# A fused linear-attention and highway kernel: two tiles per GpSimd instruction, casting value loads, sigmoid for the last nine tiles, and a new order of steps

## The chip, the cores and the metric

The kernel runs on one NeuronCore of one Trainium2 chip. The metric is device time in microseconds of one execution. Inside the profile the span is counted from the first to the last instruction or transfer of the program; the execution's own time is a little longer than its span.

The engines are named as the profile names them: PE is TensorE (matmul), DVE is VectorE, ACT is ScalarE, POOL is GpSimd and SP is SyncE, which here does nothing but issue transfers.

## What is computed

```python
def _attn_ref(q, k, v):                    # each (8, 8, 576, 64), float32
    q_s = softmax of q over the last axis  # 64 channels
    k_s = softmax of k over axis 2         # 576 positions
    kv = einsum('bhsd,bhse->bhde', k_s, v)
    return einsum('bhsd,bhde->bhse', q_s, kv)

def _moe_ref(x, w_h, w_t, b_t):            # x (4608, 512), weights (512, 512)
    H = maximum(x @ w_h, 0)
    T = 1 / (1 + exp(-(x @ w_t + b_t)))
    return T * H + (1 - T) * x

x = attention output, (batch, position) by (head, channel)
```

Both softmaxes are written here in short. The output is float32, 4608 by 512.

## The kernel before

There are eight batches. Each has 576 rows, that is four and a half tiles of 128 rows. A pair of batches is cut into five groups: two groups of two tiles for each batch, and one group of a single tile that takes the last 64 rows of both. So there are 20 groups (u = 0 to 19) and 36 tiles (i = 0 to 35).

For a batch b the steps are: load q, k and v in float32 (`q`, `k`, `v`); exponentials of k and q on ACT to 16 bit (`ek`, `eq`); a cast of v to 16 bit on ACT, DVE or POOL (`vc`); the 72 small matmuls of k by v with a column of ones beside v that gives the sum (`kv`); reciprocal and scaling (`kr`, `kn`); a swap of row blocks on PE and its copy (`kp`, `kc`); and 32 by 32 transposes of the exponentials of q on DVE (`tr`).

For a group: the product with the query side on PE (`xu`), the reciprocals of its sums (`rs`) and the scaled rows x in 16 bit (`x`), both on DVE.

For a tile: four PE transposes (`xt`) and their copy out (`xe`); the bias put into a PSUM bank (`bw`, by a PE matmul, or by an ACT copy with `:A`); four matmuls with w_t on top of it (`mt`); four matmuls with w_h into another bank (`mh`); tanh of half the gate (`th`; with `:S` it stays in PSUM); then `dd` (L391), `gg` (L396), `uu` (L405 on POOL, L402 on DVE) and `oo` (L417) make the output row, and `st` or `st1` stores it. PSUM has three banks for gate and product (`ps_g`), four for `xu` and `kv`, and one for the transposes, of which half is used.

Before the change w_h has the identity taken off and is halved (`whd`, `whc`, L202 to L210), so that `dd` is max(half of H's product, minus half x) and the gate is tanh + 1.

What sets the order of all work is `ORDER`, one list of steps written out (L16 to L57). The program walks it once, and each step issues its instructions in that place on its engine's queue. Every engine runs its own queue in this order and waits only where data or a buffer is missing. All loads of q, k, v and the weights are issued by SP (L178, L184, L189), so they lie in one queue; the bias alone is loaded from ACT's queue (L192). The list begins:

```python
q_0_0_8 b_0 setupdve fill_10 b_32 v_0_1_1 bsplit bp fill_12 bc v_0_3_1 setuppool v_0_2_1 vc_0_2_1:A vc_0_1_1:D k_0_0_2
ek_0_0_2 perm bw_0_0 v_0_0_1 vc_0_0_1:P k_0_2_2 ek_0_2_2 w_t_2 wtc_2:P eq_0_0_8 vc_0_3_1:D kv_0 kr_0 kn_0 tr_0_0_8
fill_4 kp_0 kc_0:A q_0_8_10 bw_2_0 xu_0 rs_0 x_0 fill_5 xt_1 eq_0_8_10 tr_0_8_8 bw_1_0 w_t_0 wtc_0:P w_h_0 xe_1:A
whd_1:P xu_1 w_h_2 xt_0 rs_1 whd_2:P mt_1_0 th_1_0 xe_0:D mt_0_0 k_1_2_2 v_1_2_2 vc_1_2_2:P th_0_0 gg_0_0:P x_1 xt_2
xe_2:A mt_2_0 ek_1_2_2 th_2_0 whd_0:D k_1_0_2 ek_1_0_2 whd_3:D whc_2:D tr_0_16_2 whc_0:D mh_2 dd_2 mh_1 mh_0 bw_3_0
```

`fill_n` are n matmuls on zeros. The number after a load's batch is its first part and then how many parts: a whole k, v or q of one batch is 1,152 KB, a whole weight matrix 1,024 KB.

Of the kernel before, what the change touches and what calls it, by code (L numbers as in the profile page):

```python
# [8 lines left out]
FP32 = mybir.dt.float32  # L9
FP16 = mybir.dt.float16  # L10
# [11 lines left out]
gg_2_0:P uu_2_0:P oo_2_0:P xt_3 dd_1 v_1_0_2 vc_1_0_2:A kv_1 dd_0 gg_1_0:P q_1_0_8 eq_1_0_8 xe_3:D kr_1 mh_3 q_1_8_10
kn_1 kp_1 mt_3_0 kc_1:A v_3_0_4 tr_1_0_8 xu_2 dd_3 rs_2 x_2 xt_5 uu_0_0:P oo_0_0:P eq_1_8_10 bw_5_0 tr_1_8_8 xu_3
xe_5:D rs_3 th_3_0 xt_4 gg_3_0:P uu_1_0:P tr_1_16_2 uu_3_0:P oo_1_0:P vc_3_0_2:A mt_5_0 vc_3_2_2:P xe_4:A q_3_0_18 x_3
mh_5 k_3_0_4 dd_5 bw_4_0 xt_7 th_5_0 bw_7_0 eq_3_0_8 eq_3_8_10 mt_4_0 xe_7:D tr_3_0_8 th_4_0 xu_4 rs_4 xt_6 ek_3_0_4
gg_5_0:P mt_7_0 x_4 th_7_0 uu_5_0:P mh_4 mh_7 oo_3_0:P gg_4_0:P xe_6:D kv_3 gg_7_0:P oo_5_0:D mh_6 dd_4 k_2_0_4 dd_7
# [34 lines left out]
def kernel(  # L61
# [13 lines left out]
    P = 128  # L75
# [404 lines left out]
```

## Time and profile before

| what | us |
|---|---|
| runs, median (lowest to highest) | 122.46 (122.06 to 124.19) |
| the profiled execution's own time | 122.67 |
| its span | 120.9 |
| PE, DVE, POOL, ACT busy | 104.6, 95.1, 90.1, 88.5 |

The mean granted TensorE clock was 0.979 in the profiled execution. A row of the profile's groups names the line, engine and operation, what is written and read, the shape, and how often; then the busy time, the mean length of one in ns, and the idle time before it. The list of instructions in order of time has start and length in us. A row marked SPq is the time that SP took to issue a transfer, not the transfer.

### The profile page before, as it was taken

The numbers are of one execution on the slowest core, as the hardware profiler recorded it, in microseconds if no ns is written. First come the engines' busy times: TensorE is split into PE (matmuls) and PEld (weight loads), VectorE is DVE, ScalarE is ACT, GpSimd is POOL, SyncE is SP. The second block draws the span as 40 slices with busy tenths as digits, with TensorE's granted clock in tenths as the row PEclk, the third lists the DMA queues.
The fourth block names the chain that finished last, engine by engine and source line by source line (L and its number), as shares of the span: only waits on it lengthen the run. The fifth ranks groups of instructions, "written<-read, shape, count | busy, mean of one in ns | idle before, by whom it ended". The sixth has DMA issues, their size and how long they took to land.

```text
span 120.9 us, 4081 instructions
## 1 busy us (share of the span) xinstructions
PE 104.6 (87%) x1722; PEld 53.4 (44%) x1722; DVE 95.1 (79%) x171; ACT 88.5 (73%) x120; POOL 90.1 (75%) x102
## 2 busy tenths in 40 slices
PE   6993998886798999979999999999995999999900
PEld 2241543452453654345555454564552555444500
DVE  5430588569959899999988799999988699978860
ACT  4046644986599997889999999999977687767310
POOL 7002341798999899999649998969799999848930
PEclk9999779999999999999999999999999999999997
DMA  3999999999999999999999999999996442282442
GB/s 60 387 374 408 421 395 392 392 392 403 399 391 390 402 406 400 387 393 387 406 418 400 410 394 419 397 403 409 410 371 267 160 173 96 100 329 89 173 167 96
DMA packets 14886, 40.11 MB, mean 332 GB/s; under 512 B 914, under 2 KB 1170, under 8 KB 14868
## 3 DMA queue, kind: packets, MB, share of 16 engines
q1 hardware_dynamic: 14576, 39.59, 84.9%
q8 instruction: 13, 0.21, 0.7%
q10 hardware_dynamic: 292, 0.27, 0.7%
q14 instruction: 5, 0.04, 0.1%
HBM read 30.41 MB, written 9.44 MB: 330 GB/s over the span
## 4 chain that ended last, share of the span: by engine, by line
PE 49%; DMA 26%; ACT 10%; DVE 4%; SPq 3%; issue 2%; POOLq 1%; DVEq 0%
PE tps L371 19%; PE gps L377 17%; DMA k<-in_k_dram 13%; DMA w32h<-in_moe_w_h_dram 9%; PE turned L351 5%; DMA v<-in_v_dram 4%; ACT qe L285 4%; PE kv L254 3%; PE xu L316 3%; SPq L184 3%; ACT ek L235 2%; ACT v L240 2%; PE tps L366 1%; ACT tps L384 1%; ACT xT L357 1%
## 5 line engine op out<-in xcount | busy, mean ns | idle before, releaser
L377 PE MATMUL gps<-w16h,xT 128*128 128x512 f16 x144 | 36.2, 379 | 1.3 <-issue 1.3
L371 PE MATMUL tps<-w16t,xT 128*128 128x512 f16 (+1 forms) x148 | 36.4, 374 | 0.8 <-ACT xT L357 0.8
L417 POOL TENSOR_TENSOR o<-u,x 128x512 f32<-128x512 f16 x27 | 32.4, 1209 | 0.9
L405 POOL TENSOR_TENSOR u<-g,d 128x512 f16<-128x512 f16 (+1 forms) x25 | 28.7, 1150 | 3.7 <-DVE d L391 2.0
L391 DVE SCALAR_TENSOR_TENSOR d<-x,gps 128x512 f16<-128x512 f16 x36 | 24.2, 678 | 4.5 <-PE gps L377 3.6
L344 DVE TENSOR_TENSOR x<-xu,rs 128x1024 f16<-128x1024 f32 (+1 forms) x20 | 22.2, 1112 | 0.6
L303 DVE STREAM_TRANSPOSE et<-qe 128x512 f32<-128x512 f32 (+1 forms) x24 | 19.6, 835 | 2.4 <-ACT qe L285 2.2
L235 ACT ACTIVATE ek<-k 128x2304 f16<-128x2304 f32 (+1 forms) x10 | 18.9, 1893 | 2.4 <-DMA k<-in_k_dram 2.4
L396 POOL TENSOR_SCALAR g<-th 128x512 f16<-128x512 f16 (+1 forms) x25 | 16.0, 641 | 6.0 <-ACT th L387 3.3
L285 ACT ACTIVATE qe<-q 128x1024 f16<-128x1024 f32 (+1 forms) x16 | 18.4, 1160 | 2.4 <-DVE et L303 1.8
L377 PEld LDWEIGHTS <-xT 128*128 128x128 f16 x144 | 13.0, 98 | 14.0 <-issue 1.8
L371 PEld LDWEIGHTS <-xT 128*128 128x128 f16 x148 | 13.2, 98 | 12.7 <-ACT xT L357 0.9
L387 ACT ACTIVATE th<-tps 128x512 f16<-128x512 f32 (+1 forms) x25 | 14.5, 586 | 4.3 <-PE tps L371 4.2
L357 ACT COPY xT<-turned 128x512 f16<-128x512 f16 x23 | 13.4, 583 | 5.7 <-PE turned L351 5.7
L351 PE MATMUL turned<-idh,x 128*128 128x128 f16 x144 | 14.0, 220 | 2.6 <-DVE x L344 2.3
L240 POOL CAST v<-v 128x1152 f16<-128x1152 f32 (+1 forms) x8 | 9.0, 1131 | 8.9 <-DMA v<-in_v_dram 8.9
L351 PEld LDWEIGHTS <-x 128*128 128x128 f16 x144 | 10.0, 98 | 10.1 <-DVE x L344 3.9
L165 PE MATMUL turned<-blank 128*128 128x512 f16 x31 | 10.5, 500 | 1.2 <-DVE blank L153 1.2
L364 ACT COPY tps<-ball 128x512 f32<-128x512 f32 x17 | 10.0, 591 | 0.9 <-DVE d L391 0.8
L240 ACT CAST v<-v 128x1152 f16<-128x1152 f32 (+1 forms) x8 | 8.7, 1106 | 1.5 <-DMA v<-in_v_dram 1.5
L254 PE MATMUL kv<-v,ek 64*64 64x65 f16 x576 | 6.6, 193 | 3.2 <-ACT ek L235 1.9
L402 DVE SCALAR_TENSOR_TENSOR u<-tps,d 128x512 f16<-128x512 f32 (+1 forms) x12 | 7.9, 659 | 1.5 <-ACT tps L384 1.4
(50 smaller groups left out, 92.2 us busy)
## 6 DMA issues: line engine op xcount, KB each, us to landing
out_dram<-o SPq DMA_DIRECT2D x16, 512.0 KB, 9.8
v<-in_v_dram SPq DMA_DIRECT2D x6, 1152.0 KB, 15.2
q<-in_q_dram SPq DMA_DIRECT2D x6, 1152.0 KB, 15.2
k<-in_k_dram SPq DMA_DIRECT2D x6, 1152.0 KB, 17.8
k<-in_k_dram SPq DMA_DIRECT2D x4, 576.0 KB, 8.8
q<-in_q_dram SPq DMA_DIRECT2D x2, 640.0 KB, 12.4
v<-in_v_dram SPq DMA_DIRECT2D x4, 288.0 KB, 4.7
v<-in_v_dram SPq DMA_DIRECT2D x2, 576.0 KB, 12.3
```

The source lines that it names most:

```text
L235: nc.scalar.activation(dst[:, at], src[:, at], AF.Exp)
L240: copy(v16[b % NV][:, c:c + n, :, 0:D], src[:, c:c + n])
L285: nc.scalar.activation(t[:, :, j * D:(j + n) * D], src[:, :, j * D:(j + n) * D], AF.Exp)
L303: nc.vector.transpose(dst, src)
L344: nc.vector.tensor_mul(dst[:, :, 0:n], sums(u)[:, :, :, 0:64], T[f"rs{u}"][:, :, 0:n].unsqueeze(3).to_broadcast([P, 4, n, D]))
L351: nc.tensor.matmul(t[:, n], x_of(i)[:, n0 + n % 2:n0 + 2 * P:2], idh, is_transpose=True, start=True, stop=True, skip_group_check=True)
L371: nc.tensor.matmul(T[f"tps{i}_{h}"][:, cs], T[f"xT{i}"][:, n], w16["t"][:, n, cs], start=False, stop=(n == 3), skip_group_check=True)
L377: nc.tensor.matmul(t, T[f"xT{i}"][:, n], w16["h"][:, n], start=(n == 0), stop=(n == 3), skip_group_check=True)
L391: nc.vector.scalar_tensor_tensor(t, x_of(i), -0.5, T[f"gps{i}"], op0=ALU.mult, op1=ALU.max)
L396: nc.gpsimd.tensor_scalar(t[:, cs], T[f"th{i}_{h}"][:, cs], 1.0, 1.0, op0=ALU.add, op1=ALU.mult)
L405: nc.gpsimd.tensor_mul(t[:, cs], T[f"g{i}_{h}"][:, cs], T[f"d{i}"][:, cs])
L417: eng.tensor_add(t[:, cs], T[f"u{i}_{h}"][:, cs], x_of(i)[:, cs])
```

## The change

1. GpSimd's three steps can take both tiles of a group in one instruction (`gq`, `uq`, `oq`; 128 by 1024 in place of twice 128 by 512). To this end the intermediate tiles and the transposed x are allocated in pairs, two (or three) pairs deep, and the transposes of a group's two tiles go to the two halves of their PSUM bank. Seven of the gate steps go to ACT (`gg:A`, `gq:A`).
2. The weights are cast and nothing more. `dd` is now max(H, 0) minus x, the gate is half of tanh plus a half, and from tile 27 on ACT computes the sigmoid itself, so that these tiles have no gate step. A step `tab` runs one element column of sigmoid ahead of them.
3. The values of batches 2 to 7 are loaded by GpSimd's queue in float32 to 16 bit, the cast done by the transfer, into two buffers; a block of 64 ones behind the values takes the place of the column beside them, so the matmuls of k by v move 128 columns in place of 65 for these batches.
4. The query exponentials of batches 2 to 7 are one instruction of 2304 elements each. The x of four groups is made in two halves (`x:H`, `xb`).
5. The whole list of steps is a new one. The bias goes into PSUM by ACT in 29 cases (17 before) and by PE in 8 (20 before). Transposed tiles are copied out by DVE in 20 single steps and two double ones (13 before) and by ACT in 12 (23 before). On DVE lie 7 `uu` (12 before) and 9 `oo` (10 before).

```diff
 ORDER = """
...
+q_0_0_8 b_32 b_0 setupdve fill_10 v_0_1_1 v_0_3_1 v_0_0_1 bsplit v_0_2_1 k_0_2_2 vc_0_3_1:P k_0_0_2 w_t_2 q_0_8_10
+w_t_0 k_1_2_2 v_1_0_2 vc_0_2_1:A vc_0_0_1:D ek_0_2_2 v_1_2_2 bp fill_12 k_1_0_2 ek_0_0_2 q_1_0_8 w_h_2 setuppool w_h_0
+perm bc q_1_8_10 eq_0_0_8 k_2_0_4 wc_t_2:P vc_0_1_1:D kv_0 fill_3 kr_0 kn_0 kp_0 fill_2 q_2_0_18 v_2_0_4 tr_0_0_8
+kc_0:A xu_0 rs_0 bw_1_0:A x_0 eq_0_8_10 q_3_0_18 k_3_0_4 bw_0_0 fill_5 xt_0 xe_0:D wc_t_0:A mt_0_0 vc_1_2_2:P tr_0_8_8
+ek_1_2_2 v_3_0_4 xt_1 xe_1:D xu_1 rs_1 th_0_0 x_1 mt_1_0 th_1_0 ek_1_0_2 tr_0_16_2 k_4_0_4 xt_2 xe_2:D bw_3_0 wc_h_2:P
+bw_2_0 mt_2_0 xt_3 xe_3:A eq_1_0_8 vc_1_0_2:D kv_1 kr_1 kn_1 tr_1_0_8 kp_1 kc_1:A wc_h_0:D th_2_0 mt_3_0 th_3_0 xu_2
+rs_2 x_2 gg_2_0:P mh_1 dd_1 mh_0 gq_0:A dd_0 eq_1_8_10 tr_1_8_8 mh_2 xt_4 bw_5_0:A xe_4:D gg_3_0:P xt_5 xe_5:A uq_0:P
+mh_3 dd_2 xu_3 rs_3 mt_5_0 th_5_0 x_3:H uu_2_0:P tr_1_16_2 mh_5 xb_3:H xt_6 xu_4 bw_4_0 dd_3 mh_4 dd_5 rs_4 ek_2_0_4
+xt_7 xe_6:D x_4 eq_2_0_18 mh_6 uu_3_0:P mt_4_0 th_4_0 xe_7:D dd_6 oq_0:P bw_7_0:A kv_2 v_4_0_4 xt_8 xe_8:A dd_4 mt_7_0
+th_7_0 tr_2_0_8 kr_2 kn_2 gq_2:P uq_2:P tr_2_8_8 q_4_0_18 kp_2 kc_2:A tr_2_16_2 mh_7 dd_7 xu_5 mh_8 bw_8_0:A mt_8_0
...
+xe_34:A uu_32_0:P oo_32_0:D mt_33_0 st_12 xu_19 uu_31_0:P oo_26_0:P dd_28 mh_33 st_16 oo_31_0:D uu_28_0:D rs_19
+th_33_0 mh_34 bw_34_0:A mt_34_0 th_34_0:S oo_28_0:D x_19 dd_33 dd_34 xt_35 bw_35_1 uu_27_0:P xe_35:D st1_26_0
+uu_34_0:D oo_34_0:D mh_35 dd_35 oo_27_0:P uu_33_0:P st_17 st_15 bw_35_0 oo_33_0:P mt_35_1 th_35_1:S st_18 uu_35_1:D
+oo_35_1:P st1_35_1:A mt_35_0 th_35_0:S uu_35_0:D oo_35_0:D st1_35_0:A
 """
...
+    def load_v(e, b, c, n):
+        if b < CASTS:
...
+            nc.sync.dma_start(t[:, c:c + n], rows_of(v, b)[:, c:c + n])
+            return
+        w = NJ * D
+        t = v16s[b % NVS][:, c * w:(c + n) * w].rearrange("p (c f) -> p c f", c=n)
+        nc.gpsimd.dma_start(t, rows_of(v, b)[:, c:c + n])
...
+    def w_cast(e, w, c):
+        copy = dict(A=nc.scalar.copy, D=nc.vector.tensor_copy, P=nc.gpsimd.tensor_copy)[e]
+        copy(w16[w][:, c:c + 2], T[f"w{w}{c}"])
...
+                        at, vt = (NJ * i + j) * D, v16s[b % NVS]
+                        moving = bass.AP(vt.tensor, vt[rows, at:at + D].offset,
+                                         [list(vt[rows].ap[0]), [4 * NJ * D - at, 2], [1, D]])
...
-        t = T[f"xtps{i}"] = turned[:, 0]
+        t = turned[:, tiles[i][1]]
...
+        how = dict(func=AF.Sigmoid) if i >= SIGMOID else dict(func=AF.Tanh, scale=0.5)
...
-        nc.vector.scalar_tensor_tensor(t, x_of(i), -0.5, T[f"gps{i}"], op0=ALU.mult, op1=ALU.max)
+        nc.vector.scalar_tensor_tensor(pair("d", i), T[f"gps{i}"], 0.0, x_of(i), op0=ALU.max, op1=ALU.subtract)
...
+    def halved(e, g, th):
+        if e == "A":
+            nc.scalar.activation(g, th, AF.Identity, scale=0.5, bias=half)
+        else:
+            nc.gpsimd.tensor_scalar(g, th, 0.5, 0.5, op0=ALU.mult, op1=ALU.add)
...
+    def gq(e, g):
+        halved(e, both("g", g), both("th", g))
+
+    def uq(e, g):
+        nc.gpsimd.tensor_mul(both("u", g), both("th" if groups[g][2][0] >= SIGMOID else "g", g), both("d", g))
+
+    def oq(e, g):
+        out_of(groups[g][2][0])
+        nc.gpsimd.tensor_add(T[f"oo{g}"], both("u", g), T[f"x{g}"].rearrange("p a h e -> p a (h e)"))
```

`CASTS` and `NVS` are 2 and `SIGMOID` is 27.

More of the change, by code (lines that the diff above doesn't have):

```diff
@@ L22 @@
[L22 to L26, printed above, removed]
@@ L154, in setup_dve @@
         nc.vector.memset(ones, 0.0)
+        nc.vector.memset(half, 0.5)
         nc.vector.memset(b16, 0.0)
```

189 lines of the change are left out of this document (94 added, 95 removed).

## The prediction

> **What bounds the kernel now.** I read the page's head and slices first, then the busy time in stretches of 10 us, the chain of waits, the engines' instructions in order of time, and last the groups for prices.
>
> ```profile
> PE 104.6 (87%) x1722; PEld 53.4 (44%) x1722; DVE 95.1 (79%) x171; ACT 88.5 (73%) x120; POOL 90.1 (75%) x102
> ...
> PE   6993998886798999979999999999995999999900
> ...
> DMA  3999999999999999999999999999996442282442
> ```
>
> PE is nearly full from slice 20 to 38, the transfers from slice 2 to 30. The stretches say the same, and that the other engines have little to spare either (columns: PE, PE's weight loads, DVE, ACT, POOL, clock, share of the transfer engines):
>
> ```profile
> 20.00:30.00 10.00, 7.87 (x141) 4.00 (x139) 7.57 (x16) 8.16 (x11) 7.86 (x8) 1.00 1.05 394
> 40.00:50.00 10.00, 9.53 (x206) 4.94 (x206) 8.98 (x19) 8.87 (x12) 9.56 (x10) 1.00 1.04 402
> 70.00:80.00 10.00, 10.00 (x191) 5.35 (x190) 9.64 (x18) 9.72 (x13) 8.54 (x10) 1.00 1.04 405
> ```
>
> So there are two stages: until about 40 us PE waits for what has to be loaded, afterwards it works through its list. Two loads that ACT waits for give the loading rate:
>
> ```profile
> 11.08 1.22 ACT L235 ACTIVATE ek<-k 128x1152 f16<-128x1152 f32 x1 [1.00 <-DMA k<-in_k_dram]
> 36.89 2.31 ACT L235 ACTIVATE ek<-k 128x2304 f16<-128x2304 f32 x1 [0.28 <-DMA k<-in_k_dram]
> ```
>
> In SP's order 2,816 KB end with the first, 12,416 KB with the second: 9,600 KB in 25.81 us, 372 KB/us. The chain of waits (start, length, what) gives PE's prices in the full stage, here at its densest:
>
> ```profile
> 59.62 0.71 PE kv L254 x71
> 60.32 0.97 PE tps L371 x4
> 61.30 0.22 PE turned L351 x4
> 61.52 0.12 PE kv L270 x2
> ...
> 75.39 0.36 PE xu L316 x30
> ...
> 77.81 0.22 PE turned L351 x4
> 78.03 0.86 PE gps L377 x4
> ```
>
> Four matmuls of 512 columns cost 0.86, or 0.97 behind small ones.
>
> **PE's sum before.** At 32.75 us PE has done `mt` and `mh` of tiles 0 to 3 and half of `mt_5`. Left are 63.5 times 0.863 (54.8), 31 `xt` at 0.225 (7.0), 12 `xu` at 0.36 and 4 small at 0.27 (5.4), 6 `kv` at 0.71 (4.3), 6 `kp` (0.7), 13 whole and 2 half bias matmuls at 0.22 (3.0): 75.2. PE ends at 114.76, so 82.0 us went by: 6.8 us are waits and changes of form.
>
> **PE's sum after, from the first `mh` on.** In the new list `mh_1` comes when only `mt_0` to `mt_3` and `xu_0` to `xu_2` are done. Left are 68 times 0.863 (58.7), 32 `xt` (7.2), 13 and 4 `xu` (5.8), `kp` (0.7), 3 whole and 2 half bias matmuls (0.9), and six wide `kv`. No row shows these: 0.71 if the number of matmuls sets it, 0.71 x 128/65 = 1.40 if the columns do. I take the middle, 1.05 (6.3). Sum: 79.6. The 12 bias matmuls saved (2.6) are mostly eaten by the wide `kv` (2.0).
>
> **When the first `mh` can go.** It needs both casts of w_h. The new list loads w_h behind k_1, v_1 and half of q_1: 8,320 KB in SP's queue (before: 5,504), at 372 KB/us landing at 25.9. The DVE cast (0.67) is queued ahead of `rs_2` and `x_2`, so the sums of group 2 and everything behind wait for it too.
>
> But v_2 and v_3 no longer lie in SP's queue. POOL issues v_2 behind its cast of w_t (lands at 12.40 in the trace, plus 1.04), so at about 13.5, while SP has some 4,000 KB outstanding; it issues v_3 behind its cast of v_1, at about 24.5. Neither waits for a buffer. Does a second queue wait its turn? The bias is the one case in the trace:
>
> ```profile
> 0.73 0.44 SPq L184 DMA_DIRECT2D q<-in_q_dram  x1
> 0.73 0.78 ACTq L192 DMA_DIRECT2D b<-in_moe_b_t_dram  x2
> 2.12 0.42 DVE L214 CAST b<-b 1x512 f16<-1x512 f32 x1
> ```
>
> It was read at 2.12, while the q load issued at the same moment took 3.8 us to land (the shortest of L184). It did not wait behind it. I therefore take it that the two queues share evenly: v_2 is done by 20.7, v_3 by 31.7, and both (2,304 KB, 6.2 us) stand ahead of w_h, which lands at 32.1. This is the step on which the forecast hangs. The Trainium skill, page "DMA: Bandwidth & Descriptors", section "Queues, rings and completion order", says that each transfer engine takes turns between queues packet by packet; by that rule it comes out the same, and the bias agrees as far as 2 KB can.
>
> So DVE's cast ends at 32.75, and PE, which ran dry at about 29.6 (q_1 at 27.0, its exponential 1.05, transpose 1.1, `xu_2` 0.36), starts `mh_1` there. 32.75 + 79.6 + 6.8 = 119.1 for PE's end, against 114.76. What this costs later: DVE has 13.3 us of steps from there to `xu_5`, which so comes at 46; q_2 lands at 39.9 and is no longer what ends last.
>
> **The end.** Before, 6.1 us pass from PE's end to the span's:
>
> ```profile
> 114.16 0.60 PE L371 MATMUL tps<-w16t,xT 128*128 128x256 f16 x4
> ...
> 116.90 1.36 ACTq L438 DMA_DIRECT2D out_dram<-o  x2
> ```
>
> The new list does `dd_35` ahead of the last half, so behind PE come tanh's place 0.4, `uu` 0.42, `oo` 0.42, the issue 0.7, 2.1 to land and about 0.5: 4.7. Against it POOL still has `uu_33`, `oo_33` and a half `oo`, and the 512 KB of group 18 behind them: up to 6.5. I take 5.4.
>
> **The other engines, row by row.** The nearest rows:
>
> ```profile
> L417 POOL TENSOR_TENSOR o<-u,x 128x512 f32<-128x512 f16 x27 | 32.4, 1209 | 0.9
> L405 POOL TENSOR_TENSOR u<-g,d 128x512 f16<-128x512 f16 x24 | 28.0, 1170 | 3.2 <-DVE d L391 1.5 <-DVE rz L261 0.9
> L405 POOL TENSOR_TENSOR u<-g,d 128x256 f16<-128x256 f16 x1 | 0.7, 667 | 0.5 <-DVE d L391 0.5
> L364 ACT COPY tps<-ball 128x512 f32<-128x512 f32 x17 | 10.0, 591 | 0.9 <-DVE d L391 0.8
> ```
>
> - POOL: 256 more columns cost 0.50, so some 0.16 an instruction is fixed and a double one takes 2.2 where two took 2.34. 9 `uq` 19.6, 10 `oq` 22.6, 5 `gq` 5.5, single ones 26, casts and setup 6: 80, plus six loads. A load's issue on POOL is bounded by SP's shortest (0.37) and by 3.3, one and a half double instructions; I take 1.0, the cast of half a weight matrix. 86 against 90.1, off the path (its idle time costs nothing). v_4 to v_7 wait for the `kv` that last read their buffer; `gq_2` and its like are queued behind, at moments when POOL has little queued.
> - ACT: seven value casts fewer (-8.1), eleven copies of xT fewer (-6.4), twelve bias copies more (+7.1), seven gate steps (+6.2, at the price of its other work of that width), one weight cast (+1.0), one table load (+1.3, its row at the start). Six whole exponentials of q cost 2.32 by the k row, as 1.05 + 1.27 did: nothing. About 89.5 against 88.5.
> - DVE: nine copies more (+4.3), five `uu` fewer (-3.4), one `oo` fewer (-0.9), two value casts and smaller things (+1.4): 96.5 against 95.1.
>
> All three lie beside PE's 79.6. The cover is thin: between `xu_5` and `xu_10` ACT's steps sum to 22.4, PE's to 19.4, so up to 3 us of PE's list may be uncovered there. Nine gate steps less, and transposes in two half banks, work the other way; `turned` waited for ACT's copy only 0.4 us in all. I leave the 6.8 as it is, and keep 3.5 and 10 for the range.
>
> **Sum.** Span 119.1 + 5.4 = 124.5; the profiled execution had 122.67 - 120.9 = 1.77 outside its span, so 126.3. That execution stands 0.2 above the median of the runs.
>
> **Rivals.** *The loads of v displace nothing* (they trickle, or run in the order in which they are needed): `mh_1` goes at 26.6, PE ends at 113.0, span 118.4, time 120.2. For it: the bias is only 2 KB. Against it: v_2 is issued 20 us ahead of its use with nothing to hold it. This is the rival on the other side: it decides as soon as w_h is late by less than 2.6 of the 6.2 us, for then 126.3 - 3.6 is reached. *The same with PE's waits halved* (two transpose halves, fewer gate steps, fewer tanh results that hold a PSUM bank): 116.8 to 117, so 118.5 or so; against it DVE, which is as full as PE from `xu_5` on (67 us each by rows). *A casting load takes longer for its bytes.* Before, the loads fill the transfer engines until about 85 us; six loads are 6 x 3.1 us of it. At one and a half times the price the loads end 9 us later, at twice 19 us. From `ek_7` on PE still has some 26 us, so this decides from about 1.3 times on; 130 at 1.5, 138 at 2. No row shows a cast by a transfer. *PE's clock*: between 14 and 16 us, after gaps, 0.50 was granted, so the two gaps of 3 us that I forecast before 33 may cost up to 2 us more. The Trainium skill, page "TensorE: Matmul & The Clock Gate", puts the fall to half clock after an idle window of about 3.4 us; by that rule it is a near thing, and a gap of 1.65 us at 29 us in the trace left the clock at 1.00. It is within the range of the forecast.
>
> **Chances.** Forecast 0.53 (its own range 123.9 to 129; 0.43 of it slower by over 2%, 0.10 within). Nothing displaced 0.24 (0.10 faster, 0.14 within, as 120.2 lies on the edge). Waits halved 0.11 (0.08 faster, 0.03 within). Slow cast 0.12, slower. Together faster 0.18, same 0.27, slower 0.55; 2% is about what a measurement of this kernel can tell from no change. The range leaves out the far end of the slow cast and the best of the halved waits: 119.5 to 130.
>
> **What would show it.** Right: the cast of w_h on DVE starts at about 32 and waits for its load; `rs_2` and `x_2` stand behind it; PE is idle some 3 us before 26 and again before 33; the first `gps` matmul comes at about 33 (before: 22.4); from there PE takes 86 us. Wrong: w_h at 26 (the queues do not share), the transfer engines full beyond 95 us (slow cast), or POOL rows of 2.2 us that turn out to be 1.5 or 3. A wide `kv` of 0.71 or 1.40 moves the sum by 2 us.

## The result and the profile after

| | before | after |
|---|---|---|
| runs, median (lowest to highest), us | 123.32 (122.06 to 124.19) | 131.48 (130.75 to 131.71) |
| the profiled execution's own time | 122.67 | 131.28 |
| its span | 120.9 | 129.5 |
| first matmul with w_h | 22.38 | 30.60 |
| end of PE's last matmul | 114.76 | 121.96 |

Runs more than 1.5% above the fastest run of the same kernel (here the two of 124.19) are left out of every ratio and of the medians in the table of experiments.

The ratio is 1.074 (95% interval 1.066 to 1.083): slower, as forecast, but by 8.6 us between the profiled executions and not by 3.6, and 1.5 us beyond the upper end of the range.

In the profile after, `mh` is L393, `mt` L387, `xt` L360, the copy of the transposes L369, `x` L347, `tr` L307, `eq` L289, `th` L408, `oo` L450 (L448 in the form that halves), `uq` L461, `oq` L465, the casting load L188, the cast of the weights L205, `st1` L486.

Busy time and slices of the kernel after, as the page has them:

```profile
PE 105.0 (81%) x1711; PEld 54.9 (42%) x1711; DVE 98.7 (76%) x181; ACT 88.3 (68%) x116; POOL 82.7 (64%) x69
...
PE   6590988569498998977999995999999999899600
...
DMA  3999999999999999999999999948109616406451
```

PE is busy as long as before and the span is 8.6 longer: the loss is idle time. It lies at slices 8 to 11, in gaps up to slice 25, and at the end. The transfer engines are full up to slice 26, about 84 us (before: slice 30, about 91 us). The stretches of 10 us (PE, its weight loads, DVE, ACT, POOL, clock, transfer share, GB/s):

```profile
20.00:30.00 10.00, 6.74 (x145) 3.25 (x147) 5.00 (x10) 4.67 (x8) 3.90 (x4) 0.89 1.09 331
30.00:40.00 10.00, 7.83 (x133) 4.07 (x126) 7.62 (x14) 5.35 (x7) 3.90 (x3) 0.94 1.07 374
...
70.00:80.00 10.00, 8.60 (x146) 4.51 (x144) 8.54 (x17) 8.01 (x10) 9.80 (x6) 1.00 1.08 347
```

Between 20 and 30 us every engine but PE is idle for half the time or more, PE for a third, and the transfers are full: more than before, the start waits for loads. Between 70 and 80 no engine but POOL is full and PE lacks 1.4 us: there the engines wait for each other.

**The start.** From the instructions in order of time (start, length, engine, what; in brackets the idle time before it and what ended it):

```profile
14.01 0.94 POOL L188 DMA_DIRECT2D v16s<-in_v_dram  x1
...
22.98 1.16 POOL L188 DMA_DIRECT2D v16s<-in_v_dram  x1
...
29.85 0.69 DVE L205 CAST w16h<-w32h 128x1024 f16<-128x1024 f32 x1 [1.02 <-DMA w32h<-in_moe_w_h_dram]
30.52 0.26 DVE L342 RECIPROCAL rs<-xu 128x16 f32<-128x16 f32 x1
...
30.60 3.04 PE L393 MATMUL gps<-w16h,xT 128*128 128x512 f16 x12
...
35.90 0.38 PE L360 MATMUL turned<-idh,x 128*128 128x128 f16 x4 [2.04 <-DVE xT L369]
```

The two value loads are issued about where I put them (13.5 and 24.5 forecast), DVE's cast of w_h waits for its load, and `rs_2` stands behind it. But w_h is there at 29.85, not 32.1. The queues' own rows say why (packets, MB written, share of the 16 transfer engines; q1 is SP's queue, q0 GpSimd's). Between 14 and 18 us, with the load of batch 2 issued, SP's is the only one of the two that moves anything:

```profile
q1 hardware_dynamic: 697, 1.55, 102.8%
```

Between 19 and 24 us both do:

```profile
q0 software_dynamic: 444, 0.51, 58.8%
q1 hardware_dynamic: 443, 0.93, 54.3%
```

So the two queues do share evenly, packet by packet. A packet of values is 1,152 bytes written, twice that read, about as much as one of SP's here, so the transfer time is shared about evenly too. What the forecast had wrong is when it begins. The first packet of batch 2 comes at 18.35, 3.4 us after the issuing instruction has ended, and that of batch 3 at 27.37, 3.2 after. Batch 2 (last packet at 25.19) stands wholly ahead of w_h, as forecast; of batch 3 only 197 of 528 packets have gone by 29.85. That is 3.1 + 1.2 = 4.3 us of transfers in place of 6.2, and 25.9 + 4.3 = 30.2. What passes between the issue and the first packet, no run shows. The Trainium skill, page "DMA: Bandwidth & Descriptors", section "Queues, rings and completion order", has each transfer engine go round its queues packet by packet; with both queues full that gives as many packets to one as to the other, and the trace, with 444 to 443, agrees.

PE itself waits only 1.81 us ahead of 26.29 and 0.76 ahead of 27.83 in this stretch, not twice 3.

**The middle.** From the first `mh` to its last matmul PE takes 91.36 us, 84.18 of them busy:

```profile
30.60:121.96 91.36, 84.18 (x1397) 45.33 (x1396) 82.54 (x143) 72.83 (x96) 73.87 (x50) 1.00 0.82 280
```

The kernel before has 78.65 busy of 82.0 in the corresponding stretch, 3.4 idle; here 7.2 are. The row of before:

```profile
32.75:114.76 82.01, 78.65 (x1350) 41.08 (x1348) 73.31 (x124) 69.72 (x98) 72.54 (x73) 1.00 0.86 334
```

Nearly all of the 7.2 is in ten waits of PE, of which 2.04 (above) and these are the largest:

```profile
58.81 0.38 PE L393 MATMUL gps<-w16h,xT 128*128 128x512 f16 x1 [1.23 <-DVE u L432]
...
79.12 1.04 PE L387 MATMUL tps<-w16t,xT 128*128 128x512 f16 x4 [1.40 <-ACT xT L369]
...
78.48 0.58 ACT L369 COPY xT<-turned 128x512 f16<-128x512 f16 x1 [1.83 <-DVE xT L369]
```

The last row is the copy that PE's 1.40 waits for: ACT in turn has idled for DVE's copy of the other tile of the pair.

Ahead of the 1.23 is one sum on DVE. GpSimd's and DVE's instructions at that time:

```profile
54.62 0.81 POOL L188 DMA_DIRECT2D v16s<-in_v_dram  x1 [1.40 <-PE kv L258]
55.46 2.14 POOL L465 TENSOR_TENSOR o<-u,x 128x1024 f32<-128x1024 f16 x1
...
54.92 3.24 DVE L450 TENSOR_TENSOR o<-u,x 128x512 f32<-128x512 f16 x1
58.08 0.68 DVE L432 SCALAR_TENSOR_TENSOR u<-tps,d 128x512 f16<-128x512 f32 x1
58.80 0.69 DVE L448 SCALAR_TENSOR_TENSOR o<-u,x 128x512 f32<-128x512 f16 x1
```

The sum takes 3.24 and ends 0.56 after GpSimd's double sum (57.60); a step of the same shape right behind it, with GpSimd idle, takes 0.69.

**The end.** ACT's last instructions:

```profile
121.56 0.37 ACT L408 ACTIVATE tps<-tps 128x256 f32<-128x256 f32 x1 [1.81 <-PE tps L387]
123.79 0.63 ACTq L486 DMA_DIRECT2D out_dram<-o  x1
124.52 0.37 ACT L408 ACTIVATE tps<-tps 128x256 f32<-128x256 f32 x1 [2.59 <-POOL o L450]
125.84 0.55 ACTq L486 DMA_DIRECT2D out_dram<-o  x1
...
123.09 0.67 POOL L450 TENSOR_TENSOR o<-u,x 128x256 f32<-128x256 f16 x1 [1.79 <-DVE u L430]
```

The last half's matmuls are done at 121.96, but its sigmoid comes at 124.52: in the list it stands behind the store of the other half, that store is issued by ACT, and it waits for GpSimd's sum `oo_35_1` (the last row). GpSimd has by then idled 1.79 us for DVE's `uu_35_1` (122.59), which stands behind `dd_35`.

**Prices.** Groups of the kernel after (busy time, mean ns of one, idle time before):

```profile
L465 POOL TENSOR_TENSOR o<-u,x 128x1024 f32<-128x1024 f16 x10 | 21.3, 2127 | 0.2
L461 POOL TENSOR_TENSOR u<-g,d 128x1024 f16<-128x1024 f16 x9 | 19.2, 2130 | 3.7 <-DVE d L411 2.6 <-ACT g L415 0.7
...
L289 ACT ACTIVATE qe<-q 128x2304 f16<-128x2304 f32 x6 | 12.7, 2121 | 0.0
...
L450 DVE TENSOR_TENSOR o<-u,x 128x512 f32<-128x512 f16 x6 | 8.5, 1417 | 0.1
```

The first three were forecast as 2.26, 2.18 and 2.32. DVE's sums were not: 1,417 ns in the mean, against 873 before and 680 where GpSimd leaves them alone.

### The profile page after: what moved, and what is told of

Its sections match the earlier page's. It is cut to its first block, busy times and chain, and to the rows that moved or that the text cites. A ratio compares the mean times of both kernels' runs of the same rounds, so it can differ in the third digit from the quotient of the medians.

```text
span 129.5 us, 4012 instructions
## 1 busy us (share of the span) xinstructions
PE 105.0 (81%) x1711; PEld 54.9 (42%) x1711; DVE 98.7 (76%) x181; ACT 88.3 (68%) x116; POOL 82.7 (64%) x69
## 3 DMA queue, kind: packets, MB, share of 16 engines
q0 software_dynamic: 3168, 3.54, 15.8%
## 4 chain that ended last, share of the span: by engine, by line
PE 32%; DMA 24%; DVE 20%; POOL 8%; ACT 6%; issue 5%; SPq 1%; POOLq 1%; ACTq 1%
DMA q<-in_q_dram 16%; PE gps L393 13%; PE tps L387 10%; DMA w32t<-in_moe_w_t_dram 8%; DVE o L450 5%; PE kv L258 4%; DVE x L347 4%; DVE d L411 3%; PE turned L360 3%; POOL u L428 3%; DVE et L307 3%; POOL o L450 2%; ACT ek L230 2%; PE xu L320 2%; POOL u L461 2%
## 5 line engine op out<-in xcount | busy, mean ns | idle before, releaser
L387 PE MATMUL tps<-w16t,xT 128*128 128x512 f16 (+1 forms) x148 | 37.0, 381 | 2.6 <-ACT xT L369 1.4
L393 PE MATMUL gps<-w16h,xT 128*128 128x512 f16 x144 | 35.9, 382 | 2.8 <-DVE u L432 1.2
L411 DVE SCALAR_TENSOR_TENSOR d<-gps,x 128x512 f16<-128x512 f32 x36 | 24.0, 683 | 2.2 <-PE gps L393 1.4
L408 ACT ACTIVATE th<-tps 128x512 f16<-128x512 f32 x30 | 17.8, 596 | 8.9 <-PE tps L387 8.1
L347 DVE TENSOR_TENSOR x<-xu,rs 128x1024 f16<-128x1024 f32 (+1 forms) x24 | 22.7, 950 | 0.5
L461 POOL TENSOR_TENSOR u<-g,d 128x1024 f16<-128x1024 f16 x9 | 19.2, 2130 | 3.7 <-DVE d L411 2.6
L465 POOL TENSOR_TENSOR o<-u,x 128x1024 f32<-128x1024 f16 x10 | 21.3, 2127 | 0.2
L307 DVE STREAM_TRANSPOSE et<-qe 128x512 f32<-128x512 f32 (+1 forms) x24 | 19.7, 837 | 1.0 <-ACT qe L289 1.0
L387 PEld LDWEIGHTS <-xT 128*128 128x128 f16 x148 | 13.3, 99 | 16.3 <-ACT xT L369 2.2
L393 PEld LDWEIGHTS <-xT 128*128 128x128 f16 x144 | 13.1, 98 | 16.6 <-issue 2.4
L380 ACT COPY tps<-ball 128x512 f32<-128x512 f32 x29 | 17.0, 591 | 2.6 <-DVE d L411 2.4
L289 ACT ACTIVATE qe<-q 128x2304 f16<-128x2304 f32 (+2 forms) x10 | 17.4, 1738 | 1.6 <-DMA q<-in_q_dram 1.6
L360 PE MATMUL turned<-idh,x 128*128 128x128 f16 x144 | 13.2, 219 | 2.9 <-DVE xT L369 2.4
L360 PEld LDWEIGHTS <-x 128*128 128x128 f16 x144 | 10.0, 98 | 9.1 <-issue 2.5
L428 POOL TENSOR_TENSOR u<-g,d 128x512 f16<-128x512 f16 x7 | 8.5, 1219 | 6.9 <-DVE d L411 4.7
L450 POOL TENSOR_TENSOR o<-u,x 128x512 f32<-128x512 f16 (+1 forms) x8 | 9.5, 1191 | 2.2 <-DVE u L430 1.8
L258 PEld LDWEIGHTS <-ek 64*64 64x64 f16 x576 | 7.6, 107 | 7.2 <-ACT ek L230 6.1
L369 ACT COPY xT<-turned 128x512 f16<-128x512 f16 x12 | 7.0, 585 | 5.0 <-DVE xT L369 3.1
L369 DVE COPY xT<-turned 128x512 f16<-128x512 f16 x20 | 8.2, 414 | 2.6 <-PE turned L360 1.7
```

The source lines that it names most:

```text
L289: nc.scalar.activation(t[:, :, j * D:(j + n) * D], src[:, :, j * D:(j + n) * D], AF.Exp)
L307: nc.vector.transpose(dst, src)
L347: nc.vector.tensor_mul(dst[:, :, lo:hi], sums(u)[:, :, lo:hi, 0:64], T[f"rs{u}"][:, :, lo:hi].unsqueeze(3).to_broadcast([P, 4, hi - lo, D]))
L360: nc.tensor.matmul(t[:, n], x_of(i)[:, n0 + n % 2:n0 + 2 * P:2], idh, is_transpose=True, start=True, stop=True, skip_group_check=True)
L387: nc.tensor.matmul(T[f"tps{i}_{h}"][:, cs], T[f"xT{tiles[i][0]}"][:, tiles[i][1], n], w16["t"][:, n, cs], start=False, stop=(n == 3), skip ...
L393: nc.tensor.matmul(t, T[f"xT{tiles[i][0]}"][:, tiles[i][1], n], w16["h"][:, n], start=(n == 0), stop=(n == 3), skip_group_check=True)
```

## The experiments

All times are in us; the ratio is to the kernel before on the same chip in the same set of runs, with its 95% interval. The median of the kernel before lay between 122.21 and 123.26 in the four sets.

| kernel | time | ratio | span |
|---|---|---|---|
| after | 131.48 | 1.074 (1.066 to 1.083) | 129.5 |
| late_values | 127.64 | 1.038 (1.031 to 1.046) | 125.8 |
| late_v3 | 129.62 | 1.054 (1.043 to 1.065) | 127.2 |
| tail | 129.72 | 1.055 (1.048 to 1.061) | 127.6 |
| singles | 131.37 | 1.068 (1.062 to 1.075) | 129.4 |
| late_tail | 126.29 | 1.026 (1.018 to 1.035) | 124.8 |
| lt_sum7 | 126.35 | 1.027 (1.020 to 1.034) | 124.5 |
| lt_copy18 | 125.28 | 1.019 (1.012 to 1.026) | 123.3 |
| lt_parts | 126.52 | 1.028 (1.021 to 1.035) | 124.9 |
| lc_load5 | 125.05 | 1.022 (1.017 to 1.027) | 123.4 |
| lc_load3 | 125.35 | 1.025 (1.020 to 1.029) | 123.2 |
| lc_all | 125.08 | 1.025 (1.009 to 1.042) | 123.4 |
| before_load3 | 125.41 | 1.026 (1.002 to 1.050) | 124.3 |
| lc_wh | 127.32 | 1.034 (1.025 to 1.043) | 125.6 |
| lc_wh5 | 126.77 | 1.033 (1.026 to 1.041) | 125.1 |
| lc_narrow | 123.85 | 1.011 (1.003 to 1.019) | 122.0 |

**late_values: the values of batches 2 and 3 issued behind the casts of w_h.**

```diff
-... q_2_0_18 v_2_0_4 tr_0_0_8 ... ek_1_2_2 v_3_0_4 xt_1 ... wc_h_2:P bw_2_0 ... gg_2_0:P mh_1 ...
+... q_2_0_18 tr_0_0_8 ... ek_1_2_2 xt_1 ... wc_h_2:P v_2_0_4 bw_2_0 ... gg_2_0:P v_3_0_4 mh_1 ...
```

> The changed kernel with the loads of v_2 and v_3 moved in the list: v_2 to behind GpSimd's second weight cast, v_3 to behind the gate step after it; nothing else. Theory 1 (early casting loads take half of the transfer engines from w_h and q_1): the cast of w_h on DVE starts at about 26 instead of 29.85, the first product with w_h at about 27 instead of 30.6, the wait of 2.0 us for q_1 at 34 to 36 is gone, and the time falls by 4 to 6 us, to 125.5 to 127.5. Rival (the lateness comes from where w_h stands in SP's own list, and PE's later waits eat what is won): w_h at 29 or later, or the time falls by less than 1.5 us.

127.64, that is 3.8 less, a little under what was expected. Two instructions of this kernel in order of time:

```profile
26.51 0.68 DVE L205 CAST w16h<-w32h 128x1024 f16<-128x1024 f32 x1
...
40.02 1.20 PE L258 MATMUL kv<-v16s,ek 64*64 64x128 f16 x72 [0.94 <-DMA v16s<-in_v_dram]
```

The cast of w_h comes 3.34 earlier and does not wait any more; the first `gps` matmul comes at 27.2 in place of 30.6, and PE takes 91.0 from there (91.4 in the kernel after). PE's wait behind q_1's second part is 1.02 in place of 2.04, and what is left is no wait for a load: the exponential (28.12) and the transposes (29.85) follow at once on ACT and DVE. The gain is the start, then: the loads displaced w_h as the forecast had it, by half its size. The price: batch 2's values are now late by 0.94.

**late_v3: only the values of batch 3 later.**

```diff
-... ek_1_2_2 v_3_0_4 xt_1 ... gg_2_0:P mh_1 ...
+... ek_1_2_2 xt_1 ... gg_2_0:P v_3_0_4 mh_1 ...
```

> The changed kernel with the load of v_3 alone moved, to behind the first gate step on GpSimd. Theory 1: half the dose, so w_h is cast at about 28 to 29, q_1's second part lands at about 30.5 instead of 33.1, and the time falls by 2 to 3 us, to 128.5 to 129.5. Rival: as with both loads moved, under 1 us.

129.62 (two runs, 128.99 and 130.26): 1.9 less, about what was expected. In the profiled run the first `gps` matmul comes at 29.77, 0.8 earlier than in the kernel after, and PE's wait behind q_1's second part is 0.95 in place of 2.04, 1.1 less. So the load of batch 3 costs half of the 3.8: of the 3.34 by which the two loads together held w_h's cast it makes 0.8, but the rest of it stands ahead of q_1's second part.

**tail: the last sigmoid ahead of the store.**

```diff
-... uu_35_1:D oo_35_1:P st1_35_1:A mt_35_0 th_35_0:S uu_35_0:D ...
+... uu_35_1:D oo_35_1:P mt_35_0 th_35_0:S st1_35_1:A uu_35_0:D ...
```

> The changed kernel with the end of the list reordered: the last gate matmuls and the last activation stand ahead of the store of the other half on ACT's queue; nothing else. Theory 3 (the last activation, ready at about 121.9, is held 2.6 us behind a store on ACT's queue that waits for GpSimd's last sum): it starts at about 122 instead of 124.5 and the time falls by 1.5 to 2.5 us, to 129 to 130. Rival (the end is set by the store of group 18 behind GpSimd's sums): under 0.7 us.

129.72, 1.8 less, as expected. ACT's last instructions here:

```profile
121.04 0.80 ACT L408 ACTIVATE tps<-tps 128x256 f32<-128x256 f32 x2 [1.81 <-PE tps L387]
123.27 1.28 ACTq L486 DMA_DIRECT2D out_dram<-o  x2
```

Both halves now run ahead of the store, without a wait for it between them.

**singles: GpSimd's double steps split in two.**

```diff
-... gq_2:P uq_2:P ... oq_1:P ...
+... gg_4_0:P gg_5_0:P uu_4_0:P uu_5_0:P ... oo_2_0:P oo_3_0:P ...
```

> The changed kernel with every double GpSimd instruction taken apart into two single ones in the same place. Theory 2 (a DVE sum with two SBUF inputs that meets a double GpSimd instruction stands still for its whole 2.1 us): DVE's sums fall from 1.42 us on average to under 1.1, the one of 3.24 us at 54.9 to under 2.2, and the time falls by 0.5 to 2 us. Rival A (GpSimd's 0.16 us of fixed cost an instruction counts): the time rises by 1 us or more. Rival B (neither is on the path): within 0.5 us.

131.37: no change. GpSimd's busy time is 85.6 in place of 82.7, so the double steps save it 2.9 us and the kernel nothing. And DVE's sum of tile 7 took 3.37 here too, across two single steps of GpSimd (55.22 to 57.49). It is not the length of one instruction that holds it: my theory, as put, fell. Here the sum waits until both steps are over; elsewhere in the same kernel one gets in between two steps of GpSimd that follow at once (at 108.34, 1.36 long), so the length of the run is no rule either.

**late_tail: both at once.**

> Both earlier moves at once: values of batches 2 and 3 loaded behind the cast of w_h and its neighbour, and the last activation of tile 35 ahead of the store on ACT's queue. Theory: the two losses lie in different places (before 35 us, and behind PE's last matmul), so they add: 131.5 - 3.8 - 1.8 = 125.9, between 125.4 and 126.4. Rival: PE's list is not what ends last once the tail is shorter, since GpSimd's sums of the last tiles and their store end at a fixed time behind the middle stage; then no more than the larger of the two is had, 127.0 to 127.7.

126.29: 5.2 less, where the two sum to 5.6. They lie in different places and add. What follows was tried on this kernel.

**lt_sum7: the held sum given to GpSimd.**

```diff
-... gg_8_0:A oo_7_0:D kc_3:A ...
+... gg_8_0:A oo_7_0:P kc_3:A ...
```

> As late_tail, and the output sum of tile 7 is done by GpSimd in place of DVE. On DVE it lay for 3.24 us across GpSimd's issue of a load and a double sum, where its like take 0.68. Theory: DVE's sum with both inputs in SBUF stands still while GpSimd is at work, so DVE loses 2.6 us there, PE waits 1.24 for the step behind it, and 0.3 and 0.2 more right after; without it PE gains 1.2 to 1.7, at 1.16 more on GpSimd, which idles 2 us at that place: 1.0 to 1.7 less than late_tail, 124.2 to 124.9. Rival A: PE's wait there only moves to the next late thing (DVE has been behind since 48 us by two transposes): under 0.4 less, 125.5 to 126. Rival B: GpSimd's next double product comes later by 1.2 and holds PE in turn: slower by up to 1.

126.35: nothing (rival A). GpSimd's and DVE's instructions at that time:

```profile
52.08 1.17 POOL L450 TENSOR_TENSOR o<-u,x 128x512 f32<-128x512 f16 x1
53.19 2.12 POOL L465 TENSOR_TENSOR o<-u,x 128x1024 f32<-128x1024 f16 x1
...
51.53 0.68 DVE L432 SCALAR_TENSOR_TENSOR u<-tps,d 128x512 f16<-128x512 f32 x1
52.25 3.62 DVE L448 SCALAR_TENSOR_TENSOR o<-u,x 128x512 f32<-128x512 f16 x1
```

The next step of DVE with both inputs in SBUF, which took 0.69 in the kernel after, is held in its place for 3.62. It stands through the end of one GpSimd instruction (53.25) and ends 0.56 after the second (55.31).

**lt_copy18: ACT's copy of tile 18 asked for first.**

```diff
-... xt_18 bw_18_0:A gq_7:P xu_11 rs_11 x_11 xt_19 xe_19:D th_17_0 mh_17 dd_17 xe_18:A mt_18_0 ...
+... xt_18 xe_18:A bw_18_0:A gq_7:P xu_11 rs_11 x_11 xt_19 xe_19:D th_17_0 mh_17 dd_17 mt_18_0 ...
```

> As late_tail, and ACT's copy of tile 18's transposes moved from behind tile 17's tanh to right behind its transposes. PE waited 1.40 us for this copy at 75 us, and ACT itself had idled 1.84 us, which the trace puts down to DVE's copy of tile 19, the other half of the same pair. Theory: the copy is held because the list lets DVE's copy of the pair's other half go first into a tile that both halves share; asked first, it needs only its own transposes, and PE's 1.40 goes: 1.0 to 1.4 less than late_tail, 124.5 to 124.9. Rival A: ACT waits for the bank of the transposes, which PE fills for tile 19, so that the copy ahead just makes tile 19's transposes wait, and DVE's copy, by the same 1.4: no change within 0.4. Rival B: it is the buffer of the pair that comes free late; then no change either, and the wait is named for another engine.

125.28, 1.0 less. ACT's and PE's instructions at this place:

```profile
72.49 0.58 ACT L369 COPY xT<-turned 128x512 f16<-128x512 f16 x1 [0.81 <-PE turned L360]
...
73.12 0.38 PE L360 MATMUL turned<-idh,x 128*128 128x128 f16 x4 [0.32 <-ACT xT L369]
```

The copy now waits for its own transposes only, and of PE's 1.40 there is 0.32 left, since tile 19's transposes wait for the copy of the half beside theirs. PE's wait for batch 2 at 40 us differs between the two profiled runs as well (1.53 and 0.93; 0.83 to 1.71 in the kernels with this start), so of the 1.0 in the medians some part may be that. The wait for the copy came from the change's first part: the two tiles of a group share one destination, and the list let the other half go first.

**lt_parts: the whole exponentials of q in two again.**

```diff
-... eq_2_0_18 ... eq_7_0_18 ...
+... eq_2_0_8 eq_2_8_10 ... eq_7_0_8 eq_7_8_10 ...
```

> As late_tail, and the exponentials of q of batches 2 to 7 in two instructions, 1024 and 1280 elements, as they were before the change, but both in the place of the whole one. Theory (whole exponentials cost nothing where PE waits, since PE's wait for a tanh behind one is 0.22 and its other waits are for DVE and for DVE's half of a pair): within 0.4 of late_tail, and ACT's busy time up by 6 x 0.2 = 1 us at most. Rival: the whole exponential holds the first transposes of its batch by 1.2 us each time, and these hold PE: 0.5 to 1.5 less.

126.52: no change. The whole exponentials cost nothing that shows.

**lc_load5, lc_load3, lc_all: the waits that were left, taken away one by one.**

```diff
-... kv_3 kr_3 kn_3 v_5_0_4 xe_11:A ... oq_2:P mh_9 ...
+... kv_3 kr_3 kn_3 xe_11:A ... oq_2:P v_5_0_4 mh_9 ...
```

> As lt_copy18, and GpSimd's issue of the value load of batch 5 moved from ahead of its double sum of group 2 to behind it. GpSimd idled 1.4 us ahead of that issue (it waits for the product of batch 3), so the double sum then starts 1.4 to 2.0 earlier, at about 49.9, and ends at 52.0, before or soon after DVE's sum of tile 7 begins (51.3). Theory: DVE's sums with both inputs in SBUF stand still only while GpSimd runs; the sum of tile 7 takes 1.3 in place of 3.24 if the issue of a load does not hold it, 2.1 to 2.3 if it does; PE's wait of 1.23 behind it shrinks by 1.0 to 1.2 and the end comes 0.8 to 1.2 earlier than in lt_copy18, at 124.1 to 124.5. Rival: as with the sum given to GpSimd, another step of DVE is held in its place or PE finds the next wait: within 0.4 of 125.3.

125.05: within 0.4 (the rival), although the sums are free. GpSimd's and DVE's instructions in order of time:

```profile
49.87 2.12 POOL L465 TENSOR_TENSOR o<-u,x 128x1024 f32<-128x1024 f16 x1
51.94 0.81 POOL L188 DMA_DIRECT2D v16s<-in_v_dram  x1
52.77 1.17 POOL L428 TENSOR_TENSOR u<-g,d 128x512 f16<-128x512 f16 x1
54.02 1.49 POOL L450 TENSOR_TENSOR o<-u,x 128x512 f32<-128x512 f16 x1
...
51.62 0.93 DVE L450 TENSOR_TENSOR o<-u,x 128x512 f32<-128x512 f16 x1
52.47 0.68 DVE L432 SCALAR_TENSOR_TENSOR u<-tps,d 128x512 f16<-128x512 f32 x1
53.18 1.32 DVE L448 SCALAR_TENSOR_TENSOR o<-u,x 128x512 f32<-128x512 f16 x1
```

3.24 and 0.69 became 0.93 and 1.32, 1.7 us of DVE's time, and of PE's waits there, 1.23, 0.27 and 0.17, two others came: 0.78 at 55.3 and 0.67 at 61.4.

```diff
-... gg_2_0:P v_3_0_4 mh_1 ... uu_2_0:P tr_1_16_2 ...
+... gg_2_0:P mh_1 ... uu_2_0:P v_3_0_4 tr_1_16_2 ...
```

> As lt_copy18, and the value load of batch 3 issued later, behind GpSimd's product of tile 2 (at about 33.3 in place of 27.6). In lt_copy18 the load of batch 2 took 14.3 us to land and PE waited 0.93 for it at 39.1. Theory: the two loads lie in the same queue and share its rate from 27.6 on, so that batch 2 waits for bytes of batch 3; with batch 3 later, batch 2 lands by 37 and PE's wait goes: 0.6 to 1.0 less, 124.3 to 124.7. Rival A: loads of one queue land in order of issue, and batch 2 was slow because SP's queue takes most of the rate: no change within 0.3. Rival B: batch 3 is then late for its own product at 49 us and PE waits there: slower by 0.5 to 3.

125.35: no change (rival A). With batch 3 issued at 33.3, PE waits for batch 2's values as before, 0.83 in place of 0.93, until 39.9, 14 us after their issue at 25.8. The trace shows where the 14 us go. Batch 2's first packet comes at 30.06; its 528 packets take 8.2 us beside as many of SP's (349 to 350 between 33 and 38.3 us). Batch 3's first packet comes at 38.31, right behind batch 2's last at 38.30, and in lt_copy18 it is the same (38.37 behind 38.35), though there batch 3 was issued at 27.70. So a later load of this queue does not take from the one ahead of it.

> lt_copy18 with both moves (loads of batch 5 and of batch 3 issued later) and, as a third, the second transposes of batch 1 placed behind DVE's copy of tile 4's transposes, since PE waited 0.96 for that copy at 31 us. If each of the three waits goes as the theories have it, 0.9 + 0.8 + 0.7 less: 122.9, between 122.4 and 123.6, which is no different from the kernel before. If PE's waits only move on: 124.5 to 125.3.

125.08: PE's waits moved on. Of the three, none gives what it measured.

**before_load3: one thing of the change in the kernel before.**

```diff
-... w_t_2 wtc_2:P eq_0_0_8 ... kc_1:A v_3_0_4 tr_1_0_8 ...
+... w_t_2 wtc_2:P v_3_0_4 eq_0_0_8 ... kc_1:A tr_1_0_8 ...
...
-            nc.sync.dma_start(t[:, c:c + n], rows[:, c:c + n])
+            (nc.gpsimd if (which, b) == ('v', 3) else nc.sync).dma_start(t[:, c:c + n], rows[:, c:c + n])
```

> The kernel before, with one thing of the change: the value load of batch 3 is issued by GpSimd, behind its first cast of w_t (at about 13.5), in float32 as it was, in place of by SP at 16.6 behind the loads of batch 1. Theory (two queues share the transfer engines evenly): at 13.5 SP still has 5.3 us of loads, 1,950 KB, ahead of w_h's landing; of the next 6.2 us half goes to the values, so w_h lands at 21.8 in place of 18.7, the first gps matmul comes at 25.4 in place of 22.4, and the time is 1 to 2.5 us more, since part of it goes into waits that PE has there anyway. Rival: the second queue takes only what is left over, or waits for SP's: first gps at 22.4 to 23, the time within 0.5 us. Were the cast in the transfer what delays, this kernel, which has none, would show no delay either.

Slower by 2.6%, the interval from 0.2% to 5%: the loss is there without a cast, though its size is uncertain. But not where I put it. GpSimd issues the load at 13.08, and its first packet comes at 17.36, 3.3 us after the issue has ended; in the kernel before, the two halves of w_h are there by 16.64 and 18.77. The queues' rows between 18 and 21 us, and two of ACT's instructions:

```profile
q0 software_dynamic: 175, 0.81, 69.9%
q1 hardware_dynamic: 176, 0.37, 34.7%
```

```profile
28.03 1.15 ACT L240 CAST v<-v 128x1152 f16<-128x1152 f32 x1 [0.27 <-DMA v<-in_v_dram]
29.39 1.06 ACT L285 ACTIVATE qe<-q 128x1024 f16<-128x1024 f32 x1 [0.20 <-DMA q<-in_q_dram]
```

Again one packet for one, and since a packet of values is 4,608 bytes here (0.81 MB in 175 packets), they have two thirds of the transfer time while they last. As that begins so late, w_h is late by only 0.7 to 1.3 and the first `gps` matmul not at all (21.9); the loads of batch 1, behind the values' last packet, have the full 3.3 (ACT has these two at 24.75 and 26.11 in the kernel before), and PE waits 2.5 for them.

**lc_wh, lc_wh5: w_h in its old place in SP's queue.**

```diff
-... w_t_0 k_1_2_2 ... q_1_0_8 w_h_2 setuppool w_h_0 ... xe_2:D bw_3_0 wc_h_2:P ... gg_2_0:P v_3_0_4 mh_1 dd_1 mh_0 gq_0:A dd_0 ...
+... w_t_0 w_h_2 w_h_0 k_1_2_2 ... q_1_0_8 setuppool ... wc_h_2:P vc_1_2_2:P ... x_1 wc_h_0:D ... xe_2:D mh_1 dd_1 mh_0 dd_0 bw_3_0 v_2_0_4 ... gq_0:A gg_2_0:P v_3_0_4 ...
```

> As lt_copy18, and the weights w_h loaded right behind w_t (5,504 KB into SP's queue, where the kernel before has them), their casts and the two products of tiles 0 and 1 with them earlier to match; the loads of batch 1 come 1,024 KB later. Theory: the start is still bound by what is loaded in front of PE, and the place of w_h in SP's order costs part of what is left against the kernel before: the first gps matmul at 22 to 23.5 in place of 27.3, PE gets 1.7 us of its list done while it would wait for batch 1, and the time is 0.5 to 2.0 less than lt_copy18: 123.3 to 124.8. Rival: batch 1, 2.75 us later, takes it back (its product waits for its values), and PE has done those two products but no more: within 0.4, or up to 1 slower.

127.32, against 125.28 of lt_copy18, and a ratio of 1.034 against 1.019: slower, and by more than the rival had it. PE's instructions:

```profile
22.28 1.89 PE L393 MATMUL gps<-w16h,xT 128*128 128x512 f16 x8 [0.20 <-DVE w16h L205]
26.04 0.78 PE L258 MATMUL kv<-v,ek 64*64 64x65 f16 x72 [0.35 <-ACT ek L230]
...
32.98 0.38 PE L360 MATMUL turned<-idh,x 128*128 128x128 f16 x4 [1.86 <-DVE xT L369]
```

The first `gps` matmul comes at 22.3, where the kernel before has it, and it does not help: `kv` of batch 1 comes at 26.0 in place of 23.7, and the wait that lay at 31.3 is at 33.0 and longer (1.86 in place of 0.96). So the mark that I gave in the prediction, the first `gps` matmul, does not set the time by itself.

> The one before with the value load of batch 5 issued behind the double sum too. Theory: a start that is earlier leaves the middle stage as it is, so this is lc_wh less 0.2, as lc_load5 was 0.2 less than lt_copy18. Rival: with PE earlier by a microsecond or more, the sums of DVE that stand behind GpSimd are again what ends last, and here it is worth 0.8 or more.

126.77, within the runs of lc_wh (126.10 to 127.42).

**lc_narrow: the products of k by v narrow again.**

```diff
-        n = 65 if b < CASTS else 128
+        n = 65
...
-                                         [list(vt[rows].ap[0]), [4 * NJ * D - at, 2], [1, D]])
+                                         [list(vt[rows].ap[0]), [1, D + 1]])
```

> As lt_copy18, but the products of k by v of batches 2 to 7 move 65 columns in place of 128 (64 values and one column that is the next value and not a one, so the sums of the exponentials of k of these batches are left out and their scale is wrong). A wide one takes 1.13, a narrow one 0.71: PE's list is 6 x 0.42 = 2.5 us shorter and nothing else changes. Theory (PE's list, with its waits, is what ends last from 60 us on, as I forecast): 1.6 to 2.5 less than lt_copy18, 122.8 to 123.7. Rival (PE's waits in the middle are made by DVE, ACT and GpSimd, each of which is as full, so a shorter list only makes longer waits): under 0.8 less, 124.5 to 125.3.

This kernel leaves out the sums of the exponentials of k, so it gives a price and is not one to use. 123.85; PE ends at 115.73 in place of 117.11, so 1.4 of the 2.5 that were taken off its list arrive (0.9 by the ratios). That lies between the theory and its rival: PE's list sets the end for something over half, and the rest goes into waits for the other engines.

## Why the prediction was right and wrong

Against the forecast's own steps, for the profiled execution:

| step | forecast | measured | difference |
|---|---|---|---|
| first `mh` | 32.75 | 30.60 | -2.15 |
| six wide `kv` | 6.3 | 6.8 | +0.5 |
| changes of form in PE's list | 3.4 | 4.1 | +0.7 |
| PE's waits behind the first `mh` | 3.4 | 7.2 | +3.8 |
| behind PE's last matmul | 5.4 | 7.5 | +2.1 |

(The 6.8 us of "waits and changes of form" are split by the busy time in the stretch of before: 82.0 - 78.65 = 3.4 idle, 78.65 - 75.2 = 3.4 form.) The sum is +5.0: 126.3 became 131.3.

- *The values displace w_h:* right, and late_values shows it (3.8 us). "The two queues share evenly" is right as well, packet for packet (444 to 443). What failed in this step is "both stand ahead of w_h": a load that GpSimd issues has its first packet only 3.2 to 3.5 us after the issue has ended, a term that the forecast did not have, so of batch 3 only 1.2 of its 3.1 us came ahead of w_h. That made the start 2.15 better than forecast. The bias, a load of 2 KB from ACT's queue, could not show it. And the rest of batch 3 fell on the load behind w_h, as the next point says.
- *"I leave the 6.8 as it is"* is the step that failed most. Three things were in it. The load of q_1's second part is late by the same displacing, which I counted for w_h only: its exponential waits, its transposes stand on DVE ahead of the copy of tile 4, PE waits 2.04; with late_values 1.02, with batch 3 alone moved 0.95, and that rest is the order on DVE. Second, the pairs that part 1 of the change makes tie a copy on ACT to one on DVE: 1.40, of which lt_copy18 gives back 1.0. I had read the pairs as memory and not as an order. Third, DVE's sums held behind GpSimd: 1.7 of PE's waits are marked so, but lt_sum7 and lc_load5 show that without them PE waits elsewhere, so they are not a cause of their own. I had put 3.5 to 10 for the range, and 11.3 came.
- *The end:* 5.4 was made from what lies behind PE and what GpSimd has left, side by side. In the list they lie in a row, by a store on ACT's queue that waits for GpSimd, which waits for DVE, and stands ahead of the last sigmoid. tail gives 1.8 back. For DVE's cast the prediction names what is queued behind an instruction that waits; here it does not.
- *Prices and totals:* right. POOL 82.7 (86 forecast), ACT 88.3 (89.5), DVE 98.7 (96.5); a wide `kv` 1.13 (1.05, between the two readings). Whole exponentials cost nothing (lt_parts), double steps save GpSimd 2.9 us and the kernel nothing (singles). "Off the path" holds for each total and was still the wrong conclusion: three engines at 64 to 76% with single waits of one to two us cost PE 7.
- *Rivals:* loads that displace nothing is refuted. The slow cast as well: q0 takes 15.8% of 129.5 us for 7.08 MB of float32, 2.89 us/MB, against 84.9% of 120.9 us for 39.59 MB in SP's queue before, 2.59, so 1.12 times, where it would have had to be 1.3; side by side, between 19 and 24 us, the two queues took the same (2.87 and 2.92 us a MB read). PE's clock was granted at 0.80 between 26 and 29 us and 0.63 up to 32; the twelve `gps` matmuls there took 3.04, those of the kernel before 2.75, so it cost 0.3 there (part of the 0.7 in the table) and not 2; the four `mt` matmuls from 28.00 on took 1.91, but w_h was not there yet.
- *A side remark:* the 12 bias matmuls saved (2.6) are those of the whole list; in the stretch that is summed it is ten (2.1), and the sum has it so.
- *What stays open:* mended (lt_copy18), the kernel is 1.9% slower than the one before, some 2.5 us. 0.9 to 1.4 of that is the wide `kv`. The rest, 1 to 1.6 us, goes into waits of the middle that moved on each time when one was taken away; which list would do without them was not found.

## What to carry to other kernels

Ahead of a move of loads to a second queue, take each thing that is still to land on the first one as late, not just the one that looks last; count the sharing in packets, and look for when the new queue's first packet comes, which can be well after the issue. "Waits as before" is not a forecast for a new order of steps: walk through the places where an instruction that waits has another engine's work queued behind it, the last store above all. And a wait that is named at PE is worth its length only if nothing else comes due behind it: of the three that were taken away in the middle, one was (lt_copy18, and not lt_sum7 or lc_load5).

## What the runs showed of the hardware

- GpSimd's queue beside a full SP queue moved one packet for one of SP's: 444 to 443 with a cast (19 to 24 us, kernel after), 175 to 176 without (18 to 21 us, before_load3). Its share of the transfer time went by the size of its packets: about half with the cast, two thirds without.
- The first packet of a load that GpSimd issued came 3.2 to 3.5 us after the issuing instruction had ended, in all runs, where nothing of an earlier load was left in that queue; of SP's first load it came 0.65 us after (1.83 behind 1.18). A second load in GpSimd's queue began when the first had gone (lc_load3).
- A DVE sum with both inputs in SBUF that begins while a GpSimd step runs ends 0.54 to 0.56 us after a GpSimd step does (0.68 to 3.62 us long, for 0.68 alone). The Trainium skill, page "SBUF — State Buffer", section "SBUF: two separate sides", has the two share a pair of ports that the first takes for a whole instruction. The trace agrees for the single step: in the kernel after, DVE gets in between two steps of GpSimd at 109 and 114 us, and the second of these then takes 1.60 and 1.62 in place of 1.16. But in lt_sum7 and singles the sum waited across two such steps (3.62 and 3.37), and why is open.
- In the kernel after, the sum at 54.92 began beside GpSimd's issue of a load, 0.54 ahead of its next step, and did not get in; in lc_load5 one ran while an issue went on. Whether an issue that is there first holds it is open.
- A load that casts from float32 to 16 bit took 1.12 times the transfer time of its source bytes over the whole kernel, no more side by side with SP's (2.87 to 2.92 us a MB), and 0.8 to 1.3 us of GpSimd to issue.
